# A state-space layer and a mish MLP on one core: sine tables moved behind the second mish group, two mish products moved later, a ScalarE table loaded early, identity matmuls in the head's gaps, the last output in two parts

## Chip, cores, metric

One core of one Trainium2 chip. The metric is device time of one execution in microseconds (us), the median of several executions. The span of a profile is about 2 us shorter than the time of the same execution (before: 633.1 and 635.1 us), so spans are compared with spans and times with times.

## The reference

The input x has 2048 rows of 1024. It is normalised, and the result feeds two branches: a diagonal complex state-space recurrence, and an MLP with mish.

```python
def _A_ref(x, Lambda_re, Lambda_im, B_re, B_im, C_re, C_im, log_dt, Dskip):
    Lam = Lambda_re + 1j * Lambda_im
    Bmat = B_re + 1j * B_im
    Cmat = C_re + 1j * C_im
    Lam_bar = jnp.exp(jnp.exp(log_dt) * Lam)
    B_bar = ((Lam_bar - 1.0) / Lam)[:, None] * Bmat
    Bu = jnp.einsum("bld,pd->blp", x + 0j, B_bar)
    h = jnp.zeros_like(Bu[:, 0, :]); hs = []
    for t in range(L):
        h = Lam_bar[None, :] * h + Bu[:, t, :]
        hs.append(h)
    hseq = jnp.stack(hs, 1)
    return 2.0 * jnp.einsum("blp,dp->bld", hseq, Cmat).real + x * Dskip[None, None, :]

def _B_ref(x, w1, b1, w2):            # w1: 1024 x 3584
    h = jnp.einsum("bsd,df->bsf", x, w1) + b1
    sp = jnp.log1p(jnp.exp(-jnp.abs(h))) + jnp.where(h > 0, h, jnp.zeros_like(h))
    return jnp.einsum("bsf,fd->bsd", h * jnp.tanh(sp), w2)

xn = _layernorm(x, axis=-1)
out = x + _A_ref(xn, ...) + _B_ref(xn, ...)
```

## The kernel before

The kernel goes through four blocks of 512 rows. In each block TensorE does four stages:

1. w1: 28 tiles of 8 matmuls. VectorE evicts each tile to `hb` and adds the bias.
2. Projection with B: 8 tiles of 16 matmuls. VectorE evicts each by multiplying it with sine and cosine tables (`tab`), which turns the complex recurrence into a real one.
3. w2: 224 matmuls that accumulate in all eight PSUM banks.
4. Projection with C: 128 matmuls into the same banks. It needs the recurrences, which VectorE does meanwhile.

ScalarE computes mish in four groups of seven tiles: exp, ln, tanh over 3584 columns each. VectorE multiplies the result with `hb` (`mish_mul`), which also frees `hb` for later tiles. In the first block there is extra work: layernorm without a predecessor to hide behind (the head), the sine tables, and the coefficients.

In the traces here each of these engines starts its operations in the order in which the program lists them: in the kernel before, the first mish exp (39.09 us) starts only behind the third sine table (35.65 us) that the code lists before it. So the place of a call in the code is read below as its place in its engine's queue.

```python
NWARM = 34
for i in range(NWARM):            # identity matmuls, result not used
    PE.mm(lambda e: e.matmul(ps[:, 4, 0:P], lhsT=ident[:], rhs=ident[:], start=True, stop=True), ...)
PE.op(lambda e: e.transpose(ps16(5)[:, 0:NST], st[:, :], ident[0:NST, 0:NST]), ...)   # parameters
for h in range(2):
    first_sums_v(0, h)            # VectorE: statistics of rows 0 to 127 (quarter 0)
first_var_v(0)
vop(lambda e: e.tensor_copy(par[:, :], ps16(5)[:, 0:NST]), ...)
first_mean_a(1)                   # ScalarE: mean of quarter 1
first_rsqrt(0)                    # ScalarE
first_var_a(1)
first_rsqrt(1)
first_sums_v(2, 0)
first_apply(0)                    # VectorE: Newton step, then xn
first_transpose(0)                # TensorE
first_apply(1)
first_transpose(1)
first_copy(0, VE)                 # PSUM to xnT
first_mean_a(3)
first_var_a(3)
first_rsqrt(3)
first_copy(1, AC)                 # on ScalarE
# ... quarters 2 and 3
for f in range(NSPLIT):           # first halves (256 columns) of w1 tiles 0 to 5
    first_half(f, 0)
    if f in (1, 3):
        q = 2 + f // 2
        first_transpose(q)
        first_copy(q, AC if q == 2 else VE)
# ... POOL: phases(j), the arguments of the sines, one j after the other

def table(j):                     # ScalarE
    src, b_src = ph_slot(j)       # written by POOL
    aop(lambda e: e.activation(tab[:, 1, j, :], src[:], AF.Sin, ...), ...)
    aop(lambda e: e.activation(src[:], src[:], AF.Abs), ...)
    aop(lambda e: e.activation(tab[:, 0, j, :], src[:], AF.Sin, ...), ...)

def first_tile(blk, f):           # ... matmuls of w1 tile f
    if f % GF == 0 and f >= 2 * GF:
        mish_mul(f // GF - 2)     # VectorE
    vop(lambda e: e.tensor_scalar(hb[:, hs, :], ps[:, bank, :], b1(f), None, op0=ALU.add), ...)
    if f % GF == GF - 1:
        mish(f // GF)             # ScalarE

def project_in(blk):
    for j in range(NJ):           # banks 4-5, 6-7, 0-1, 2-3, and again
        # ... 16 matmuls, two multiplications with tab, a sum and a difference on VectorE
        if j == 4:
            mish_mul(2)
        if j == 7:
            mish_mul(3)

def tail(blk):
    # ... w2: six f for banks 4 to 7 first, then all; C; then for each quarter q:
    vop(lambda e, q=q, xr=xr: e.tensor_tensor(xr, ps[:, 2 * q:2 * q + 2, :]..., xr, op=ALU.add), ...)
    AC.dma(lambda e, xr=xr, r0=r0: e.dma_start(out[0, r0:r0 + P, :], xr), ...)

def side(f):                      # first block, behind w1 tile f
    if f == 5:
        for j in range(3):
            table(j)
    if f == 13:
        for j in range(3, NJ):
            table(j)
    # ... coefficients, next block's layernorm
    if f < 16 and f % 2 == 0:
        transpose_B(f // 2)       # transposed loads, SP's queue
    if f >= 16:
        transpose_C(f - 16)
```

Of the kernel before, what the change touches and what calls it, by code (L numbers as in the profile page):

```python
# [5 lines left out]
ALU = mybir.AluOpType  # L6
AF = mybir.ActivationFunctionType
DT = mybir.dt

P = 128  # L10
# [146 lines left out]
def build_kernel(nc, A_x, A_Lambda_re, A_Lambda_im, A_B_re, A_B_im, A_C_re, A_C_im,  # L157
# [24 lines left out]
        return nc.alloc_sbuf_tensor(name, shape, dtype)  # L182


    NWARM = 34
    NRING = 7
    ring = sb("ring", [P, NRING, 2048], bf16)
    b_ring = [Buf("ring%d" % i) for i in range(NRING)]
# [18 lines left out]
    tab = sb("tab", [P, 2, NJ, TB], bf16)  # L207
    b_tab = [Buf("tab%d" % j) for j in range(NJ)]
    xx = sb("xx", [P, 2, NQ, D], bf16)
    b_xx = [[Buf("xx%d_%d" % (i, q)) for q in range(NQ)] for i in range(2)]  # L210
    s_xx = [[DmaSem(nc, "d_xx%d_%d" % (i, q)) for q in range(NQ)] for i in range(2)]
    xn = sb("xn", [P, NQ, D], bf16)
    b_xn = [Buf("xn%d" % q) for q in range(NQ)]
# [37 lines left out]
    def ps16(i):  # L251
        return ps[:, i, :].bitcast(bf16)
# [86 lines left out]
    def first_sums_v(q, h):  # L339
        s = q // 2  # L340
        vop(lambda e: e.bn_stats(stats[:, s, h, :], xx[:, 0, q, h * 512:(h + 1) * 512]),
            reads=[b_xx[0][q]], writes=[b_stats[s]])
# [37 lines left out]
    def first_transpose(q):  # L380
        bank = 6 + q % 2
        for k in range(NK):
            PE.mm(lambda e, k=k: e.transpose(ps16(bank)[:, k * P:(k + 1) * P], xn[:, q, k * P:(k + 1) * P], ident[:]),
                  reads=[b_xn[q], b_ident], writes=[b_ps[bank]], first=k == 0, last=k == NK - 1)

    def first_copy(q, queue):
        dst = xnT[:, :, q * P:(q + 1) * P]
        srcp = ps16(6 + q % 2).rearrange("p (k t) -> p k t", k=NK)
        if queue is AC:
            aop(lambda e: e.copy(dst, srcp), reads=[b_ps[6 + q % 2]], writes=[b_xnT[q]])  # L390
        else:
            vop(lambda e: e.tensor_copy(dst, srcp), reads=[b_ps[6 + q % 2]], writes=[b_xnT[q]])
# [60 lines left out]
            reads=[b_cs[in0]], writes=[b_cs[out_]])  # L453


    for i in range(NWARM):
        PE.mm(lambda e: e.matmul(ps[:, 4, 0:P], lhsT=ident[:], rhs=ident[:], start=True, stop=True),
              reads=[b_ident], writes=[b_ps[4]], first=i == 0, last=i == NWARM - 1)
    PE.op(lambda e: e.transpose(ps16(5)[:, 0:NST], st[:, :], ident[0:NST, 0:NST]),
          reads=[b_st, b_ident], writes=[b_ps[5]])  # L460
    for h in range(2):
        first_sums_v(0, h)
    first_var_v(0)
    vop(lambda e: e.tensor_copy(par[:, :], ps16(5)[:, 0:NST]), reads=[b_ps[5]], writes=[b_par])
    first_mean_a(1)
    first_rsqrt(0)
    first_var_a(1)
    first_rsqrt(1)
    first_sums_v(2, 0)
    first_apply(0)  # L470
    first_transpose(0)
    first_apply(1)
    first_transpose(1)
    first_copy(0, VE)
    first_mean_a(3)
    first_var_a(3)
    first_rsqrt(3)
    first_copy(1, AC)
    first_sums_v(2, 1)
    first_var_v(2)  # L480
    first_rsqrt(2)
    first_apply(2)
    first_apply(3)
    NSPLIT = 6

    def first_half(f, half):
# [8 lines left out]

    for f in range(NSPLIT):
        first_half(f, 0)
        if f in (1, 3):
            q = 2 + f // 2
            first_transpose(q)  # L500
            first_copy(q, AC if q == 2 else VE)

# [145 lines left out]
    def project_in(blk):  # L648
        for j in range(NJ):
            bank = banks_of(j)  # L650
            for ci in range(2):
                for k in range(NK):
                    PE.mm(lambda e, j=j, ci=ci, k=k, bank=bank: e.matmul(  # L653
                        ps[:, bank + ci, :], lhsT=BT[:, ci, j, k, :], rhs=xnT[:, k, :], start=k == 0, stop=k == NK - 1),
                        reads=[b_BT[j]] + b_xnT, writes=[b_ps[bank + ci]], first=k == 0, last=k == NK - 1)
            u = ps[:, bank:bank + 2, :]
            for s in range(2):
                vop(lambda e, s=s, u=u, j=j: e.tensor_tensor(  # L658
                    mt[:, s, :, :], u, tab[:, s, j, :].unsqueeze(1).to_broadcast([P, 2, TB]), op=ALU.mult),
                    reads=[b_ps[bank], b_ps[bank + 1], b_tab[j]], writes=[b_m[s]])  # L660
            vop(lambda e, j=j: e.tensor_tensor(hT[:, 0, j, :], mt[:, 0, 0, :], mt[:, 1, 1, :], op=ALU.add),
                reads=b_m, writes=[b_hT[0][j]])
            vop(lambda e, j=j: e.tensor_tensor(hT[:, 1, j, :], mt[:, 0, 1, :], mt[:, 1, 0, :], op=ALU.subtract),
                reads=b_m, writes=[b_hT[1][j]])
            if j == 4:
                mish_mul(2)
            if j == 7:
                mish_mul(3)

    def recur(blk, j):  # L670
# [30 lines left out]
    def tail(blk):  # L701
        first = [True] * 8

        def acc(u, lhsT, rhs, reads, last=False):
            st_ = first[u]
            first[u] = False
            PE.mm(lambda e: e.matmul(ps[:, u, :], lhsT=lhsT, rhs=rhs, start=st_, stop=last),  # L707
                  reads=reads, writes=[b_ps[u]], first=st_, last=last)

        def dense(f, s, units):  # L710
            wt = ring[:, s, :].rearrange("p (f d) -> p f d", f=2)
            for u in units:
                q, h = u // 2, u % 2
                acc(u, act[:, f, q * P:(q + 1) * P], wt[:, f % 2, h * TB:(h + 1) * TB], [b_actf[f], b_ring[s]])

        def proj(j, ci, u, last):
            q, h = u // 2, u % 2
            acc(u, hT[:, ci, j, q * P:(q + 1) * P], CT[:, ci, j, h * TB:(h + 1) * TB], [b_hT[ci][j], b_CT[j]], last)

        njt = 1 if blk == 0 else 3  # L720
        base = n_item[0]
        for f in range(6):
            dense(f, (base + f // 2) % NRING, (4, 5, 6, 7))
        for f in range(NF):
            dense(f, (base + f // 2) % NRING, (0, 1, 2, 3) if f < 6 else range(8))
            if f % 2 == 1:
                item_done()
            if blk + 1 < NB and f in (7, 9, 11, 13):
                transpose_dma((f - 7) // 2)
        for j in range(NJ - njt):  # L730
            for ci in range(2):
                for u in range(8):
                    proj(j, ci, u, False)
        i = blk % 2
        for q in range(NQ):
            for j in range(NJ - njt, NJ):
                for ci in range(2):
                    for u in (2 * q, 2 * q + 1):
                        proj(j, ci, u, j == NJ - 1 and ci == 1)
            xr = xx[:, i, q, :]  # L740
            vop(lambda e, q=q, xr=xr: e.tensor_tensor(  # L741
                xr, ps[:, 2 * q:2 * q + 2, :].rearrange("p a t -> p (a t)"), xr, op=ALU.add),
                reads=[b_ps[2 * q], b_ps[2 * q + 1], b_xx[i][q]], writes=[b_xx[i][q]])
            r0 = blk * TB + q * P
            out_events[i, q] = AC.dma(lambda e, xr=xr, r0=r0: e.dma_start(out[0, r0:r0 + P, :], xr), s_out[i][q],
                                      reads=[b_xx[i][q]])
        if blk + 2 < NB:
            for q in range(NQ):
                load_x(PO, blk + 2, q)


    for blk in range(NB):
        def side(f):
            if blk:
                if f in (8, 10, 12, 15):
                    ln_skip(blk, (8, 10, 12, 15).index(f))
                return
            if f == 5:
                for j in range(3):
                    table(j)  # L760
            if f == 13:
                for j in range(3, NJ):
                    table(j)
            if f in (7, 8, 9, 10):
                coefficients(f - 7)
            if f in (9, 11, 12, 13):
                ln_skip(0, (9, 11, 12, 13).index(f))
            if f in (14, 16, 18, 20):
                ln_stats_only(1, (f - 14) // 2)
            if f == 22:  # L770
                ln_rsqrt()
            if f in (23, 24, 25, 26):
                ln_scale(1, f - 23)
            if f < 16 and f % 2 == 0:
                transpose_B(f // 2)
            if f >= 16:
                transpose_C(f - 16)

        for f in range(NF):
            first_tile(blk, f)  # L780
            side(f)
        if blk == 0:
            for i in range(12, 2 * NK):
                transpose_C(i)
        project_in(blk)
        if 0 < blk < NB - 1:
            for q in range(NQ):
                ln_stats_only(blk + 1, q)
            ln_rsqrt()
            for q in range(NQ):  # L790
                ln_scale(blk + 1, q)
        for j in range(NJ):
            recur(blk, j)
            if blk == 0:
                scale_C(j)
        if blk + 1 < NB:
            carry()
        tail(blk)
# [51 lines left out]
```

## Time and profile before

634.95 us (634.46 to 635.81, 3 runs). TensorE is busy nearly throughout; these are the first two lines of section 1 of the page (span; busy us, share of the span, instructions):

```profile
span 633.1 us, 7295 instructions
PE 614.8 (97%) x2875; PEld 286.8 (45%) x2931; DVE 463.6 (73%) x693; ACT 249.6 (39%) x163; POOL 48.5 (8%) x47
```

The Trainium skill ("Trainium Kernel Development and Optimization", Performance Expectations) calls matmul busy time a bad metric, because matmuls are pipelined. Here one matmul's record is 0.379 us long, but they start 0.2158 us apart. This is the timeline of TensorE in the kernel before (start, length of a run of like instructions, source line, operands, count; in brackets the idle time before and what ended it):

```profile
8.70 1.03 PE L383 MATMUL ps<-ident,xn 128*128 128x128 bf16 x8 [2.67 <-DVE rs L369]
10.21 1.04 PE L383 MATMUL ps<-ident,xn 128*128 128x128 bf16 x8 [0.48 <-DVE xn L376]
12.81 3.57 PE L491 MATMUL ps<-xnT,ring 128*128 128x256 bf16 x16 [1.56 <-ACT xnT L390]
16.18 0.87 PE L383 MATMUL ps<-ident,xn 128*128 128x128 bf16 x8
...
19.08 7.15 PE L491 MATMUL ps<-xnT,ring 128*128 128x256 bf16 x64
26.28 27.57 PE L633 MATMUL ps<-xnT,ring 128*128 128x512 bf16 x125
54.40 1.89 PE L633 MATMUL ps<-xnT,ring 128*128 128x512 bf16 x8 [0.55 <-issue]
56.55 8.81 PE L633 MATMUL ps<-xnT,ring 128*128 128x512 bf16 x39 [0.26 <-DVE hb L640]
65.19 1.89 PE L653 MATMUL ps<-xnT,BT 128*128 128x512 bf16 x8
67.47 3.63 PE L653 MATMUL ps<-xnT,BT 128*128 128x512 bf16 x16 [0.39 <-DVE hb L640]
71.88 22.39 PE L653 MATMUL ps<-xnT,BT 128*128 128x512 bf16 x101 [0.79 <-DVE hb L640]
94.11 0.59 PE L707 MATMUL ps<-ring,act 128*128 128x512 bf16 x2
96.44 5.35 PE L707 MATMUL ps<-ring,act 128*128 128x512 bf16 x24 [1.73 <-DVE mt L658]
102.95 42.91 PE L707 MATMUL ps<-ring,act 128*128 128x512 bf16 x194 [1.15 <-DVE mt L658]
145.69 27.79 PE L707 MATMUL ps<-CT,hT 128*128 128x512 bf16 x125
```

Read it from above. Two of the four layernorm transposes (L383) come late and slowly, 1.03 us for eight. The first 16 half-width matmuls (L491) take 0.21 us each; later ones take 0.11. The slow ones run at half clock ("cold" below, against the full, "warm" clock): the packed trace's first record of the full clock is at 16.71 us, in the run of transposes that starts at 16.18. Some counts are a few short (125 of 128), because matmul records can be missing. All gaps of TensorE behind the head are in this list; they end at 102.95 us.

The cause of the gaps in the w1 stage stands on ScalarE and VectorE (timeline of the kernel before):

```profile
35.65 0.72 ACT L523 ACTIVATE tab<-ph_h,kon 128x512 bf16<-128x512 f32 x1 [2.94 <-POOL ph_h L517]
...
37.80 1.28 ACT L611 ACT_TABLE_LOAD   x1
39.09 3.19 ACT L611 ACTIVATE act<-hb 128x3584 bf16<-128x3584 bf16 x1
...
51.32 2.12 DVE L618 TENSOR_TENSOR act<-act,hb 128x3584 bf16<-128x3584 bf16 x1 [5.28 <-ACT act L613]
```

The third sine table waits for POOL's phases until 35.65. The first mish group's exp (L611) stands behind it in ScalarE's queue and starts at 39.09. So VectorE waits 5.28 us for the first mish product (L618), and every eviction behind that is late.

Two single lines complete the picture: the second ScalarE table load in the head, and the last add of the kernel, behind which the last output still has to land.

```profile
5.75 1.28 ACT L362 ACT_TABLE_LOAD   x1
...
629.36 1.23 DVE L741 TENSOR_TENSOR xx<-ps,xx 128x1024 bf16<-128x1024 f32 x1 [1.37 <-PE ps L707]
```

### The profile page before, as it was taken

How to read it: one execution, taken by the hardware profiler on the slowest of the kernel's cores; microseconds unless marked ns; L12 is line 12 of the kernel's file. 1: busy time of each engine (PE TensorE's matmuls, PEld its weight loads, DVE VectorE, ACT ScalarE, POOL GpSimd, SP SyncE). 2: the span in 40 equal slices, each digit the busy share in tenths (PEclk: the TensorE clock that was granted, in tenths of full speed). 3: DMA queues.
4: the chain of work that ended last, by engine and by line, in shares of the span. 5: the costliest groups of instructions: out<-in, count | busy, mean ns of one | idle time of the engine just before them, and what ended most of it. 6: DMA issues, size and time to landing. Idle time of an engine off the chain costs nothing.

```text
span 633.1 us, 7295 instructions
## 1 busy us (share of the span) xinstructions
PE 614.8 (97%) x2875; PEld 286.8 (45%) x2931; DVE 463.6 (73%) x693; ACT 249.6 (39%) x163; POOL 48.5 (8%) x47
## 2 busy tenths in 40 slices
PE   5999998999999999999999999999999999999997
PEld 4744443444444444444444444444444444444443
DVE  5587999999558579999145759999714756999603
ACT  6489996442029980000006994000000999000000
POOL 1699000000010000000010000000000000000000
PEclk9999999999999999999999999999999999999999
DMA  9999992852074500575045540186304442032001
GB/s 256 214 221 232 267 191 87 215 164 67 17 237 147 165 35 0 161 206 161 6 154 155 155 134 1 38 217 179 99 30 133 139 164 67 1 132 101 0 1 66
DMA packets 124043, 79.39 MB, mean 125 GB/s; under 512 B 48874, under 2 KB 106218, under 8 KB 124010
## 3 DMA queue, kind: packets, MB, share of 16 engines
q1 hardware_dynamic: 120656, 71.58, 42.6%
q10 hardware_dynamic: 2394, 4.21, 1.8%
q0 software_dynamic: 960, 3.15, 1.8%
q8 instruction: 23, 0.38, 0.2%
q14 instruction: 10, 0.08, 0.1%
HBM read 63.19 MB, written 4.19 MB: 106 GB/s over the span
## 4 chain that ended last, share of the span: by engine, by line
PE 84%; DVE 6%; ACT 5%; POOL 2%; issue 1%; DMA 0%; SPq 0%; DVEq 0%; POOLq 0%
PE ps L707 48%; PE ps L633 21%; PE ps L653 14%; DVE mt L658 2%; ACT act L613 1%; ACT act L611 1%; ACT act L612 1%; DVE hb L640 1%; POOL py L515 1%; PE ps L491 1%; POOL px L513 1%; DVE act L618 1%; POOL ph_h L517 1%; DMA xx<-in_A_x_dram 0%; ACT L612 0%
## 5 line engine op out<-in xcount | busy, mean ns | idle before, releaser
L707 PE MATMUL ps<-ring,act 128*128 128x512 bf16 x880 | 193.5, 379 | 3.7 <-DVE mt L658 2.9
L633 PE MATMUL ps<-xnT,ring 128*128 128x512 bf16 x832 | 183.0, 379 | 1.6 <-issue 0.5
L611 ACT ACTIVATE act<-hb 128x3584 bf16<-128x3584 bf16 x16 | 50.9, 3182 | 238.3 <-DVE hb L640 238.0
L707 PEld LDWEIGHTS ps<-ring,act 128*128 128x128 bf16 x896 | 87.5, 98 | 109.1 <-DVE mt L658 3.9
L633 PEld LDWEIGHTS ps<-xnT,ring 128*128 128x128 bf16 x848 | 82.8, 98 | 101.1 <-issue 1.0
L640 DVE TENSOR_SCALAR hb<-ps,par 128x512 bf16<-128x512 f32 x112 | 82.8, 747 | 56.3 <-PE ps L633 54.3
L653 PE MATMUL ps<-xnT,BT 128*128 128x512 bf16 x500 | 110.7, 379 | 1.8 <-DVE hb L640 1.2
L707 PE MATMUL ps<-CT,hT 128*128 128x512 bf16 x500 | 110.5, 379 | 0.6
L658 DVE TENSOR_TENSOR mt<-ps,tab 128x1024 bf16<-128x1024 f32 x64 | 75.3, 1218 | 13.1 <-PE ps L653 11.6
L653 PEld LDWEIGHTS ps<-xnT,BT 128*128 128x128 bf16 x512 | 49.9, 98 | 61.9 <-DVE hb L640 1.9
L707 PEld LDWEIGHTS ps<-CT,hT 128*128 128x128 bf16 x512 | 50.1, 98 | 60.4
L741 DVE TENSOR_TENSOR xx<-ps,xx 128x1024 bf16<-128x1024 f32 x16 | 19.3, 1223 | 72.8 <-PE ps L707 72.8
L673 DVE TENSOR_TENSOR_SCAN hT<-cs,qi,hT 128x512 bf16<-128x512 f32 x48 | 58.9, 1267 | 0.0
L612 ACT ACTIVATE act<-act 128x3584 bf16<-128x3584 bf16 x16 | 51.0, 3190 | 0.2
L613 ACT ACTIVATE act<-act 128x3584 bf16<-128x3584 bf16 x16 | 51.0, 3190 | 0.2
L678 DVE TENSOR_TENSOR mt<-hT,tab 128x1024 bf16<-128x1024 bf16 x64 | 41.4, 688 | 1.1
L618 DVE TENSOR_TENSOR act<-act,hb 128x3584 bf16<-128x3584 bf16 x16 | 32.6, 2040 | 6.6 <-ACT act L613 6.6
L287 POOL DMA_DIRECT2D xx<-in_A_x_dram x12 | 6.7, 560 | 260.9 <-DVE xx L741 255.6
L587 ACT ACTIVATE ct<-CT,cs 128x512 f32<-128x512 bf16 x16 | 11.5, 720 | 31.6 <-DVE CT L589 28.4
L612 ACT ACT_TABLE_LOAD x16 | 20.5, 1283 | 0.3
L613 ACT ACT_TABLE_LOAD x16 | 20.5, 1283 | 0.3
L673 DVE TENSOR_TENSOR_SCAN hT<-cs,hT 128x512 bf16<-128x512 f32 x16 | 18.7, 1208 | 0.0
(82 smaller groups left out, 277.1 us busy)
## 6 DMA issues: line engine op xcount, KB each, us to landing
ring<-in_B_w_dram SPq DMA_DIRECT2D x112, 512.0 KB, 3.8
out_dram<-xx ACTq DMA_DIRECT2D x16, 256.0 KB, 2.0
xx<-in_A_x_dram POOLq DMA_DIRECT2D x12, 256.0 KB, 5.2
xx<-in_A_x_dram SPq DMA_DIRECT2D x4, 256.0 KB, 3.7
dsk<-in_A_Dskip_dram SPq DMA_DIRECT2D x1, 256.0 KB, 6.4
xnT<-xn SPq DMA_TRANSPOSE x12, 4.5
BT<-in_A_B_re_dram SPq DMA_TRANSPOSE x8, 6.1
BT<-in_A_B_im_dram SPq DMA_TRANSPOSE x8, 4.1
```

Source lines behind the costliest of these rows:

```text
L611: aop(lambda e: e.activation(a, hs, AF.Exp), reads=[b_hb[g % 2]], writes=[b_act[g]])
L612: aop(lambda e: e.activation(a, a, AF.Ln, bias=1.0), reads=[b_act[g]], writes=[b_act[g]])
L613: aop(lambda e: e.activation(a, a, AF.Tanh), reads=[b_act[g]], writes=[b_act[g]])
L618: vop(lambda e: e.tensor_tensor(a, a, hs, op=ALU.mult), reads=[b_act[g], b_hb[g % 2]], writes=[b_act[g]])
L633: PE.mm(lambda e, k=k: e.matmul(ps[:, bank, :], lhsT=wt[:, k, fi * P:(fi + 1) * P], rhs=xnT[:, k, :], start=k == 0, stop=k == NK - 1), rea ...
L640: vop(lambda e: e.tensor_scalar(hb[:, hs, :], ps[:, bank, :], b1(f), None, op0=ALU.add), reads=[b_ps[bank], b_par], writes=[b_hbf[hs]])
L653: PE.mm(lambda e, j=j, ci=ci, k=k, bank=bank: e.matmul(ps[:, bank + ci, :], lhsT=BT[:, ci, j, k, :], rhs=xnT[:, k, :], start=k == 0, stop= ...
L658: vop(lambda e, s=s, u=u, j=j: e.tensor_tensor(mt[:, s, :, :], u, tab[:, s, j, :].unsqueeze(1).to_broadcast([P, 2, TB]), op=ALU.mult), rea ...
L673: vop(lambda e, ci=ci, init=init: e.tensor_tensor_scan(out=hT[:, ci, j, :], data0=cj("r", j).to_broadcast([P, TB]), data1=hT[:, ci, j, :], ...
L678: vop(lambda e, s=s: e.tensor_tensor(mt[:, s, :, :], hT[:, :, j, :], tab[:, s, j, :].unsqueeze(1).to_broadcast([P, 2, TB]), op=ALU.mult), ...
L707: PE.mm(lambda e: e.matmul(ps[:, u, :], lhsT=lhsT, rhs=rhs, start=st_, stop=last), reads=reads, writes=[b_ps[u]], first=st_, last=last)
L741: vop(lambda e, q=q, xr=xr: e.tensor_tensor(xr, ps[:, 2 * q:2 * q + 2, :].rearrange("p a t -> p (a t)"), xr, op=ALU.add), reads=[b_ps[2 * ...
```

## The change

Its parts, each with its intent:

- an operation on constants at the start loads the ScalarE table that rsqrt needs while x is still coming (the other layernorm functions are in it too);
- 16, 6 and 8 identity matmuls fill gaps between the transposes, to keep TensorE's clock up;
- the parameter copy leaves the front of VectorE's queue; the second transpose's copy goes to VectorE; the transposes of quarters 2 and 3 move by one or no tile;
- all eight sine tables go behind the second mish group, so that the first group need not wait for POOL;
- in the first block the third mish product moves from behind projection tile 4 to behind tile 6, and the fourth from behind tile 7 to behind the first recurrence;
- the last output unit is finished in two halves.

```diff
-    for i in range(NWARM):
-        PE.mm(...identity...)
+    def keep_busy(n):
+        for i in range(n):
+            PE.mm(...identity...)
+
+    keep_busy(34)
     PE.op(lambda e: e.transpose(ps16(5)[:, 0:NST], st[:, :], ident[0:NST, 0:NST]), ...)
+    keep_busy(16)
+    aop(lambda e: e.activation(rs[:, :, 3], kon[:, 2:3].to_broadcast([P, NQ]), AF.Abs_reciprocal_sqrt, bias=kon[:, 2:3]),
+        reads=[b_kon], writes=b_rs)
     for h in range(2):
         first_sums_v(0, h)
     first_var_v(0)
-    vop(lambda e: e.tensor_copy(par[:, :], ps16(5)[:, 0:NST]), reads=[b_ps[5]], writes=[b_par])
+    first_sums_v(2, 0)
     first_mean_a(1)
     first_rsqrt(0)
     first_var_a(1)
     first_rsqrt(1)
-    first_sums_v(2, 0)
     first_apply(0)
     first_transpose(0)
+    keep_busy(6)
     first_apply(1)
     first_transpose(1)
+    keep_busy(8)
     first_copy(0, VE)
+    first_copy(1, VE)
     first_mean_a(3)
     first_var_a(3)
     first_rsqrt(3)
-    first_copy(1, AC)
     ...
     first_apply(3)
+    vop(lambda e: e.tensor_copy(par[:, :], ps16(5)[:, 0:NST]), reads=[b_ps[5]], writes=[b_par])
     ...
-        if f in (1, 3):
-            q = 2 + f // 2
+        if f in (2, 3):
+            q = f
     ...
-            if j == 4:
+            if j == (6 if blk == 0 else 4):
                 mish_mul(2)
-            if j == 7:
+            if j == 7 and blk:
                 mish_mul(3)
     ...
         for q in range(NQ):
-            (all matmuls of both banks, one add of 1024 columns, one output DMA)
+            units = [(2 * q, 2 * q + 1)]
+            if blk == NB - 1 and q == NQ - 1:
+                units = [(2 * q,), (2 * q + 1,)]
+            (per unit: its matmuls, its add, its output DMA)
     ...
-            if f == 5:
-                for j in range(3):
-                    table(j)
             if f == 13:
-                for j in range(3, NJ):
+                for j in range(NJ):
                     table(j)
     ...
             recur(blk, j)
+            if blk == 0 and j == 0:
+                mish_mul(3)
```

More of the change, by code (lines that the diff above doesn't have):

```diff
@@ L182, in sb @@
         return nc.alloc_sbuf_tensor(name, shape, dtype)
-    NWARM = 34
     NRING = 7
@@ L209, in build_kernel @@
     xx = sb("xx", [P, 2, NQ, D], bf16)
-    b_xx = [[Buf("xx%d_%d" % (i, q)) for q in range(NQ)] for i in range(2)]
+    b_xx = [[Buf("xx%d_%d" % (i, q), parts=[Buf("xx%d_%d_%d" % (i, q, h)) for h in range(2)])
+             for q in range(NQ)] for i in range(2)]
     s_xx = [[DmaSem(nc, "d_xx%d_%d" % (i, q)) for q in range(NQ)] for i in range(2)]
@@ L453, in smalls @@
             reads=[b_cs[in0]], writes=[b_cs[out_]])
-    for i in range(NWARM):
-        PE.mm(lambda e: e.matmul(ps[:, 4, 0:P], lhsT=ident[:], rhs=ident[:], start=True, stop=True),
-              reads=[b_ident], writes=[b_ps[4]], first=i == 0, last=i == NWARM - 1)
+    def keep_busy(n):
+        for i in range(n):
+            PE.mm(lambda e: e.matmul(ps[:, 4, 0:P], lhsT=ident[:], rhs=ident[:], start=True, stop=True),
+                  reads=[b_ident], writes=[b_ps[4]], first=i == 0, last=i == n - 1)
+    keep_busy(34)
     PE.op(lambda e: e.transpose(ps16(5)[:, 0:NST], st[:, :], ident[0:NST, 0:NST]),
           reads=[b_st, b_ident], writes=[b_ps[5]])
+    keep_busy(16)
+    aop(lambda e: e.activation(rs[:, :, 3], kon[:, 2:3].to_broadcast([P, NQ]), AF.Abs_reciprocal_sqrt, bias=kon[:, 2:3]),
+        reads=[b_kon], writes=b_rs)
     for h in range(2):
@@ L734, in tail, with finish @@
         i = blk % 2
-        for q in range(NQ):
-            for j in range(NJ - njt, NJ):
-                for ci in range(2):
-                    for u in (2 * q, 2 * q + 1):
-                        proj(j, ci, u, j == NJ - 1 and ci == 1)
-            xr = xx[:, i, q, :]
-            vop(lambda e, q=q, xr=xr: e.tensor_tensor(
-                xr, ps[:, 2 * q:2 * q + 2, :].rearrange("p a t -> p (a t)"), xr, op=ALU.add),
-                reads=[b_ps[2 * q], b_ps[2 * q + 1], b_xx[i][q]], writes=[b_xx[i][q]])
-            r0 = blk * TB + q * P
-            out_events[i, q] = AC.dma(lambda e, xr=xr, r0=r0: e.dma_start(out[0, r0:r0 + P, :], xr), s_out[i][q],
-                                      reads=[b_xx[i][q]])
+        def finish(q, lo, hi):
+            xr = xx[:, i, q, lo:hi]
+            bank, r0 = 2 * q + lo // TB, blk * TB + q * P
+            b_x = b_xx[i][q].parts[lo // TB] if hi - lo <= TB else b_xx[i][q]
+            if hi - lo > TB:
+                src, b_src = ps[:, bank:bank + 2, :].rearrange("p a t -> p (a t)"), b_ps[bank:bank + 2]
+            else:
+                src, b_src = ps[:, bank, lo % TB:lo % TB + hi - lo], b_ps[bank:bank + 1]
+            vop(lambda e: e.tensor_tensor(xr, src, xr, op=ALU.add), reads=b_src + [b_x], writes=[b_x])
+            sem = s_out[i][q] if hi - lo > TB else DmaSem(nc, "d_end%d" % lo)
+            out_events[i, q, lo] = AC.dma(lambda e: e.dma_start(out[0, r0:r0 + P, lo:hi], xr), sem, reads=[b_x])
+        for q in range(NQ):
+            units = [(2 * q, 2 * q + 1)]
+            if blk == NB - 1 and q == NQ - 1:
+                units = [(2 * q,), (2 * q + 1,)]
+            for us in units:
+                for j in range(NJ - njt, NJ):
+                    for ci in range(2):
+                        for u in us:
+                            proj(j, ci, u, j == NJ - 1 and ci == 1)
+                if len(us) == 1:
+                    finish(q, (us[0] % 2) * TB, (us[0] % 2 + 1) * TB)
+            if len(units) == 1:
+                finish(q, 0, D)
         if blk + 2 < NB:
```

## The prediction

> **What bounds the kernel now.** TensorE. The page gives PE 97% of a 633.1 us span, clock 9 tenths or more throughout; the chain of waits is 84% PE. A block has 704 matmuls of 512 columns; in the chain's steady stretches 50 take 10.79 us (49 are recorded), 215.8 ns each, so the 2816 need 607.7 us. The other 25.4 us are all there is to win (estimate from the PE timeline):
> - head: first real matmul at 12.81 us;
> - cold clock: the first 16 half-width matmuls take 3.57 us, later ones 0.112 each: 1.7 lost; identity transposes 1.3;
> - PE gaps in the first block: 0.55 and 0.26 (54 to 57 us), 0.39 and 0.79 (67 to 72), 1.73 and 1.15 (94 to 103); 4.9 us, about 5.9 with a pipeline drain each;
> - end: 3.7 from the last matmul (629.36).
> Blocks 1 to 3 have no gaps.
>
> **The change, costed.**
> 1. Head. ScalarE's chain decides it (mean, variance, rsqrt up to 11.77 in the chain of waits). Its second table load (5.75, 1.28 us) stands before rsqrt; the change loads once, at 2.49, while x is coming. The Trainium skill, "ScalarE: Activation LUTs", What ACT_TABLE_LOAD costs, gives 1283 ns; the trace agrees. VectorE no longer waits 0.62 us for the parameter copy, and the second transpose's copy moves from ScalarE (queued to 11.68, 0.99 us) to VectorE (0.68). First matmul at 10.9: -1.9.
> 2. Identity matmuls. The Trainium skill, "TensorE: Matmul & The Clock Gate", Part 1, says the full clock comes after about 3.4 us of sustained activity; here it comes at about 16.4, 3.6 us after 12.81. If the fillers hold PE busy from 5.8 to 10.9, the first halves run warm: -1.7. First halves end near 17.3 instead of 20.85: -3.5 together.
> 3. Sine tables. Three tables wait for POOL's phases (25.5, 30.5, 35.6), so the first mish group starts at 37.8 though its input is ready at 28.7. VectorE then idles 5.28 us at the first mish product (51.3), later evictions are late, and the gaps at 54 to 57 and 67 to 72 follow. After: mish 0 at 25 to 37, mish 1 to 53, eight tables (2.03 each) to 71, mish 2 and 3 to 96 (before 100.6). These four gaps should vanish: -2.6.
> 4. The third product (2.02 us at 92.1) stands between two projection evictions and causes the gaps at 94 to 103. Moved later: -2.2, about 0.9 left, since VectorE (3.26 us per tile against 3.45 on PE) starts late.
> 5. End: the last add is 1.23 us on 1024 columns; half of it hides: -0.6.
>
> Against it: w1 loads in the first block are near the DMA's limit (DMA share about 1 from 24 to 66 us). The last is issued at 54.98 and needed at 61.7; PE will want it near 57. The DMA stream starts up to 2.9 us earlier (SP waited that long at 22.8), so 0 to 1.5 us may come back as a wait for DMA. The block-1 x loads may hold VectorE a little. I take off 0.8.
>
> Sum: -3.5 -2.6 -2.2 -0.6 +0.8 = -8.1.
>
> **Predicted: 627.0 us (range 624.8 to 630.2).** Faster by over 2%: 0.02; within 2%: 0.97; slower: 0.01.
>
> **What would show it.** First w1 matmul near 10.9; its 16 halves in about 1.9 us; one table load before the exp; first mish exp near 25; no VectorE idle over 3 us at the first product; w1 stage ending near 60.5 instead of 65.2; PE gaps in the first block under 1.5 us; a last add near 0.65.
>
> **What would make it wrong.** The fillers do not reach the warm clock (+1.7) or delay the transposes; PE waits for w1 loads or for VectorE's backlog (up to +3); the third product now delays the last projection evictions. All gaps gone would give 625.

## The result, and the profile after

626.04 us (625.92 to 626.63, 4 runs), against 634.98 us before (634.46 to 635.81, 4 runs). The ratio is 0.986, 95% interval 0.9843 to 0.9877. The profiled span is 623.9 us, 9.2 us shorter.

Section 1 of the page, and the timeline of TensorE after:

```profile
span 623.9 us, 7415 instructions
PE 616.7 (99%) x2961; PEld 287.4 (46%) x2961; DVE 466.0 (75%) x695; ACT 247.1 (40%) x162; POOL 50.0 (8%) x47
```

```profile
7.41 0.62 PE L383 MATMUL ps<-ident,xn 128*128 128x128 bf16 x8 [0.50 <-DVE rs L369]
7.87 0.50 PE L458 MATMUL ps<-ident 128*128 128x128 bf16 x6
8.77 0.62 PE L383 MATMUL ps<-ident,xn 128*128 128x128 bf16 x8 [0.40 <-DVE xn L376]
9.23 0.61 PE L458 MATMUL ps<-ident 128*128 128x128 bf16 x8
10.27 2.78 PE L499 MATMUL ps<-xnT,ring 128*128 128x256 bf16 x24 [0.43 <-DVE xnT L392]
...
21.64 38.15 PE L641 MATMUL ps<-xnT,ring 128*128 128x512 bf16 x176
59.62 27.79 PE L661 MATMUL ps<-xnT,BT 128*128 128x512 bf16 x128
87.25 5.78 PE L715 MATMUL ps<-ring,act 128*128 128x512 bf16 x26
94.55 42.91 PE L715 MATMUL ps<-ring,act 128*128 128x512 bf16 x198 [1.52 <-DVE mt L666]
137.29 27.79 PE L715 MATMUL ps<-CT,hT 128*128 128x512 bf16 x128
```

The transposes take 0.62 us instead of 1.03 (the clock is up), and the first weight matmul starts at 10.27. The w1 stage and the B projection run without a gap. One gap is left behind the head, 1.52 us in front of 94.55.

The other engines' lines that answer to those shown of before:

```profile
2.43 1.28 ACT L465 ACT_TABLE_LOAD   x1 [2.43 <-issue]
...
24.35 3.19 ACT L619 ACTIVATE act<-hb 128x3584 bf16<-128x3584 bf16 x1 [4.74 <-DVE hb L648]
...
41.33 2.01 DVE L626 TENSOR_TENSOR act<-act,hb 128x3584 bf16<-128x3584 bf16 x1
...
90.21 2.02 DVE L626 TENSOR_TENSOR act<-act,hb 128x3584 bf16<-128x3584 bf16 x1
92.14 2.35 DVE L666 TENSOR_TENSOR mt<-ps,tab 128x1024 bf16<-128x1024 f32 x2
...
620.96 0.69 DVE L752 TENSOR_TENSOR xx<-ps,xx 128x512 bf16<-128x512 f32 x1 [0.60 <-PE ps L715]
```

The first mish exp starts at 24.35 instead of 39.09. VectorE reaches the first product at 41.33 and finds it ready. The third product runs at 90.21, and behind it the eviction of the last projection tile ends at 94.49 (92.14 plus 2.35); TensorE goes on at 94.55. The last add is 0.69 us.

The difference splits at the starts of the stages, all read from the two timelines:

| stretch | before, us | after, us | difference | predicted |
|---|---|---|---|---|
| start to the first weight matmul | 12.81 | 10.27 | -2.54 | -1.9 |
| from there to the first full-width w1 matmul | 13.47 | 11.37 | -2.10 | -1.7 |
| w1 | 38.91 | 37.98 | -0.93 | -2.6 with the next |
| projection with B | 28.92 | 27.63 | -1.29 | |
| w2 of the first block | 51.58 | 50.04 | -1.54 | -2.2 |
| C of the first block to the last add | 483.67 | 483.67 | 0.00 | 0 |
| last add to the end | 3.74 | 2.94 | -0.80 | -0.6 |
| PE waiting for w1 loads, given back | | | 0 | +0.8 |
| sum | | | -9.20 | -8.1 (rounded) |

The time was inside the range. What the terms don't show is why the middle three moved, and whether the head's parts add up. The experiments are about that.

### The profile page after: what moved, and what is told of

Same layout as the page of the kernel before. It is cut to its first block, busy times and chain, and to the rows that moved or that the text cites. A ratio compares the mean times of both kernels' runs of the same rounds, so it can differ in the third digit from the quotient of the medians.

```text
span 623.9 us, 7415 instructions
## 1 busy us (share of the span) xinstructions
PE 616.7 (99%) x2961; PEld 287.4 (46%) x2961; DVE 466.0 (75%) x695; ACT 247.1 (40%) x162; POOL 50.0 (8%) x47
## 4 chain that ended last, share of the span: by engine, by line
PE 95%; DVE 3%; DMA 1%; issue 0%; SPq 0%; DVEq 0%
PE ps L715 48%; PE ps L641 29%; PE ps L661 16%; DVE mt L666 2%; PE ps L499 2%; DMA xx<-in_A_x_dram 1%; DVE hT L669 0%; PE ps L383 0%; DVE hT L671 0%; DVE xn L376 0%; SPq L287 0%; DVE xnT L392 0%; DVE xx L752 0%; DVE rs L371 0%; DVE stats L341 0%
## 5 line engine op out<-in xcount | busy, mean ns | idle before, releaser
L752 DVE TENSOR_TENSOR xx<-ps,xx 128x1024 bf16<-128x1024 f32 (+1 forms) x17 | 19.5, 1161 | 72.0 <-PE ps L715 72.0
L620 ACT ACT_TABLE_LOAD x16 | 20.5, 1283 | 0.3
L621 ACT ACT_TABLE_LOAD x16 | 20.5, 1283 | 0.3
```

Source lines behind the costliest of these rows:

```text
L620: aop(lambda e: e.activation(a, a, AF.Ln, bias=1.0), reads=[b_act[g]], writes=[b_act[g]])
L621: aop(lambda e: e.activation(a, a, AF.Tanh), reads=[b_act[g]], writes=[b_act[g]])
L752: vop(lambda e: e.tensor_tensor(xr, src, xr, op=ALU.add), reads=b_src + [b_x], writes=[b_x])
```

## The experiments

Two theories of the middle, from the first w1 matmul at full width to the first C matmul (119.41 us before, 115.65 after: -3.76):

- **P**, as predicted: the sine tables account for the w1 and B stretches; the moved products account for the w2 stretch.
- **R**, formed from the trace after: TensorE waits last for the eviction of the last projection tile (banks 2 and 3). That eviction is at the end of a queue in which VectorE never idles (the trace of after has no wait of VectorE from 62 to 96 us), so only the amount of work ahead of it and the moment at which VectorE gets to it count. The third product is ahead of the last tile at its old place and at its new one. Then the tables account for everything.

Each run was timed beside the kernel before (medians of the same rounds 635.1 to 635.6 us). All were correct. Differences "in the trace" compare profiled spans or stretches of them.

| run | edit to | median, us (range) | ratio to before (95%) | profiled span |
|---|---|---|---|---|
| tables_back | after | 631.00 (630.84 to 633.26) | 0.9943 (0.992 to 0.9965) | 629.1 |
| tables_only | before | 631.41 (631.26 to 632.16) | 0.9941 (0.9927 to 0.9956) | 630.2 |
| products_back | after | 626.59 (626.02 to 626.92) | 0.9862 (0.9847 to 0.9877) | 623.9 |
| no_fill | after | 628.72 (627.90 to 629.63) | 0.9897 (0.9882 to 0.9912) | 625.9 |
| no_load | after | 628.27 (627.68 to 628.78) | 0.9889 (0.9874 to 0.9904) | 626.4 |
| fill_only | before | 634.05 (633.18 to 634.99) | 0.9981 (0.9965 to 0.9997) | 633.0 |
| load_only | before | 633.48 (633.03 to 634.08) | 0.9973 (0.9959 to 0.9988) | 632.1 |
| copy_back | after | 627.09 (627.00 to 632.09) | 0.9897 (0.9854 to 0.9939) | 625.0 |
| no_split | after | 627.60 (627.10 to 628.17) | 0.9879 (0.9865 to 0.9894) | 626.0 |
| after_again | none | 626.01 (625.95 to 626.29) | 0.9857 (0.984 to 0.9873) | 624.0 |
| product_late | after | 625.03 (624.19 to 626.45) | 0.9842 (0.9824 to 0.986) | 622.6 |
| late_and_loads | after | 624.51 (624.17 to 624.78) | 0.983 (0.9816 to 0.9843) | 622.2 |

### tables_back: the tables at their old places in the kernel after

```diff
+            if f == 5:
+                for j in range(3):
+                    table(j)
             if f == 13:
-                for j in range(NJ):
+                for j in range(3, NJ):
                     table(j)
```

> The kernel after, with three sine tables again before the first mish group and five after the second. Two theories of the gain between the first full-width w1 matmul and the first projection of C (3.8 us in the traces). Theory R, formed from the trace of after: all of it comes from the tables, since what PE waits for last is the last projection tile's eviction, and that is late only because VectorE's w1 evictions were; then +3.8 us, span about 627.7, and a PE gap of 3 us or more in all before the last projection banks. Theory P, as predicted: the tables give only the gaps at 54 to 57 and 67 to 72 us, so +2.2 us, span about 626.1, and the rest stays with the moved products.

The middle took 120.22 us instead of 115.65 (22.33 to 142.55 in its timeline): +4.57. The gaps of the w1 and B stages are back (1.31, 0.26, 0.39 and 0.78 us), and the gap in front of the last banks is 2.92 us. That is more than even R said, and far from P's 2.2. The surplus has a likely source, which these two numbers suggest and no run tests. The shorter head does not shorten POOL's chain as much: ScalarE gets the third table's phases 10.22 us behind the first full-width matmul here and 9.37 us in the kernel before (32.55 less 22.33; 35.65 less 26.28). So in the shortened head the old order would have cost more than it did. The rest of the 5.2 us of span is a first full-width matmul that came 0.69 us later in this execution. The slowest of the four runs (633.26 us) was not traced.

### tables_only: the tables alone moved in the kernel before

> The kernel before, with all eight sine tables behind the second mish group and nothing else changed (the products stay at their old places). Theory R (the tables carry the whole gain of the middle): PE gaps between 54 and 72 us gone, and those before the last projection banks down to about 1.5 us in sum: -3.8 us, span about 629.3. Theory P, as predicted (tables -2.6, the moved products the rest): -2.6 us or less, span 630.5 or more.

The edit is the reverse of the one above. The middle took 115.86 us (26.88 to 142.74) instead of 119.41: -3.55 of the -3.76, with the products at their old places. The gaps of the w1 and B stages are gone, and those before the last banks are 0.62 and 1.15 us. The time fell by 3.9 us. R holds; P is outside.

### products_back: the products at their old places in the kernel after

```diff
-            if j == (6 if blk == 0 else 4):
+            if j == 4:
                 mish_mul(2)
-            if j == 7 and blk:
+            if j == 7:
                 mish_mul(3)
     ...
-            if blk == 0 and j == 0:
-                mish_mul(3)
```

> The kernel after, with the third and fourth mish products of the first block at their old places (after projection tiles 4 and 7). Theory P, as predicted: the third product again stands before the eviction of tile 5, and PE loses about 1.5 us more: span about 625.4. Theory R: the third product is before the last tile's eviction at either place, so the evictions end at the same time; the PE gap before the last banks is split in two (about 0.6 and 0.9 us) but its sum stays 1.5 us: span 623.9, within 0.2.

The profiled span is 623.9 us, as after, and the median is 0.5 us higher with overlapping ranges. TensorE goes on with banks 2 and 3 at the same moment as after (94.63 here, 94.55 after). These are the two lines of TensorE around it, and VectorE's third product and last tile's eviction, from the timelines:

```profile
87.40 6.07 PE L715 MATMUL ps<-ring,act 128*128 128x512 bf16 x26
94.63 42.91 PE L715 MATMUL ps<-ring,act 128*128 128x512 bf16 x194 [1.16 <-DVE mt L666]
...
83.78 2.02 DVE L626 TENSOR_TENSOR act<-act,hb 128x3584 bf16<-128x3584 bf16 x1
...
92.22 2.35 DVE L666 TENSOR_TENSOR mt<-ps,tab 128x1024 bf16<-128x1024 f32 x2
```

The product starts 6.43 us earlier than after (83.78 against 90.21), and the last eviction ends at 94.57 against 94.49. So in the traces moving the products, as the change does it, is worth nothing, and Theory P's term for it was wrong. Not traced are the other three executions, with spans of 624.6 to 624.8 us, where seven of the eight executions of after (its repeat included) have 623.9 to 624.2; whether their heads or the products made that is open. What R said in detail is half shown: the recorded gap is 1.16 us instead of 1.52, and the 26 matmuls ahead of it take 6.07 us instead of 5.78, which is where the first of R's two gaps would be.

### no_fill: without the added identity matmuls

```diff
-    keep_busy(16)
-    keep_busy(6)
-    keep_busy(8)
```

(each at its place; the 34 stay)

> The kernel after, without the 16, 6 and 8 added identity matmuls. My theory (the fillers bring the full clock before the first weight matmul): the first 16 half-width matmuls are cold again (about 3.5 us instead of 1.9) and the transposes take about 1.0 us instead of 0.62, so about +2.1 us against the kernel after (span about 626.0). Rival (the 34 old identity matmuls and the earlier start of work warm the clock anyway, the head's gain is ScalarE's alone): within 0.3 us of the kernel after.

The first 24 half-width matmuls took 4.43 us instead of 2.78, the first two groups of transposes 1.03 each instead of 0.62, and the first weight matmul came at 10.66. Span +2.0, median +2.7. In the packed traces the first record of the full clock is at 14.08 us here and at 6.48 after. The fillers do bring the clock. The rival is out.

### no_load: without the early table load

```diff
-    aop(lambda e: e.activation(rs[:, :, 3], ..., AF.Abs_reciprocal_sqrt, bias=kon[:, 2:3]), ...)
```

> The kernel after, without the early ScalarE operation that loads layernorm's table. My theory: a second table load of 1.28 us returns in front of the first rsqrt, and everything behind it in the head moves: first weight matmul at about 11.5 instead of 10.27, +1.3 us (span about 625.2), more only if the longer hole between fillers and transposes costs the clock. Rival (the fillers and VectorE's order made the head's gain; the load hides behind the wait for x): within 0.3 us of the kernel after.

The first rsqrt started at 6.98 instead of 5.62 us, so the load costs 1.36 us. But the first weight matmul moved by 1.73 us and the span by 2.5, and the clock was lost on the way (timeline of TensorE; its idle times are called holes below):

```profile
8.63 0.62 PE L383 MATMUL ps<-ident,xn 128*128 128x128 bf16 x8 [1.35 <-DVE rs L369]
9.09 0.50 PE L458 MATMUL ps<-ident 128*128 128x128 bf16 x6
10.15 0.98 PE L383 MATMUL ps<-ident,xn 128*128 128x128 bf16 x8 [0.56 <-DVE xn L376]
10.92 1.06 PE L458 MATMUL ps<-ident 128*128 128x128 bf16 x8
12.00 3.58 PE L497 MATMUL ps<-xnT,ring 128*128 128x256 bf16 x24
```

The first transposes are still fast. Behind holes of 1.35 and 0.56 us the second ones are slow, the fillers take 1.06 us for 8, and the 24 halves begin slowly. The record of the granted clock agrees: it is 0.50 from 10.25 to 13.66 us and full before and after. In these traces, then, the table load and the fillers work together: the load shortens the hole in front of the first transposes from 1.35 to 0.50 us. That the holes cause the fall is an inference; copy_back below kept the clock over a hole of 1.53 us.

### fill_only and load_only: each alone in the kernel before

> The kernel before, with the 16, 6 and 8 identity matmuls and nothing else changed. Theory of the window (the clock falls back when the holes between them are too long, as the run without the early table load showed with a hole of 1.35 us): the holes stay long here, so only part of the cold time is saved: -0.3 to -1.2 us, and the second transposes take about 1.0 us again. Rival (the fillers' worth does not depend on the rest): -2.0 us, as much as taking them from the kernel after cost.

> The kernel before, with the early load of layernorm's ScalarE table and nothing else changed. If the load's 1.28 us stand on the head's chain by themselves: first weight matmul at about 11.5 instead of 12.81, -1.3 us, the first 16 half-width matmuls still cold at 3.57. Rival (VectorE's wait for the parameter copy, 0.62 us, or ScalarE's queue takes it back): -0.7 us or less.

Fillers alone: in the profiled run the hole in front of the first transposes is 1.72 us, the second transposes take 1.04 us and the first 16 halves 3.57, exactly as before, so nothing was saved in it (span 633.0). The clock had come at 6.54 us, fell to 0.50 at 9.95 and returned at 16.78. The four spans fall in two pairs, 631.2 and 631.3, 632.8 and 633.0. The better pair was not traced; that the clock held longer in it is an inference, and the mean clocks don't separate the pairs (0.996 twice; 0.995 and 0.997). The median is 1.3 us lower: short of the rival's -2.0, and also just outside the theory's -1.2. Two of the four runs (633.18 and 633.36 us) did save the rival's 2 us. So the interaction is shown in the traced execution only; the fillers alone help in some executions and not in others.

The load alone: first weight matmul at 11.38 (-1.43), the halves cold at 3.57. The median fell by 1.6 us and the profiled span by 1.0. That the span fell by less than the head fits the clock, which came 5.04 us behind the first weight matmul in that run (16.42) and 3.90 behind it in before; the second 16 halves took 2.31 us instead of 1.91. As expected; the rival is out.

### copy_back: the second copy on ScalarE again

```diff
     first_copy(0, VE)
-    first_copy(1, VE)
     ...
     first_rsqrt(3)
+    first_copy(1, AC)
```

> The kernel after, with the second transpose's copy on ScalarE behind the fourth quarter's rsqrt again. As predicted (the copy's own 0.31 us and its place in ScalarE's queue): first weight matmul at about 11.4 instead of 10.27, +1.1 us; if the hole that this leaves behind the fillers (about 1.5 us) loses the clock, up to +2. Rival (the copy is not what the first matmul waits for): 0.

First weight matmul at 11.42 (+1.15), span 625.0 (+1.1), median +1.05. The hole of 1.53 us behind the fillers did not lose the clock this time: the 24 halves took 2.78 us. One of the four runs took 632.09 us; it has no trace here, so its cause is open.

The head's parts don't add up to its gain. Taken out of after, one at a time, the fillers, the load and the copy cost 2.7, 2.2 and 1.05 us in medians, 6.0 together, and the whole head gained 4.64 us in the traces: the same clock is counted in more than one of them. The new places of the parameter copy and of the transposes were not tested alone.

### no_split: the last output in one piece

```diff
-            if blk == NB - 1 and q == NQ - 1:
+            if False:
```

> The kernel after, with the last output unit in one piece again. As predicted: the last add is 1.23 us instead of 0.69 behind the last matmul, +0.6; with the larger last transfer (2.0 us to landing instead of 1.7) +0.8, as the traces of before and after differ at the end; span about 624.7. Rival (the end is bound by the transfers in the queue before it): 0.

From the last add's start to the end it took 3.80 us (622.20 to 626.0) instead of 2.94, so the split is worth 0.86 us. The whole span is 2.1 us longer, not 0.8. The rest is another head: in this execution the third quarter of x came late (VectorE waited 0.82 us for it), the clock came late (first record of the full clock at 10.84 us, 6.48 after), and the first weight matmul was at 11.50. Such differences of the head between executions are a reason to read a part's worth from its own stretch.

### after_again, product_late, late_and_loads: the last gap

R says that the remaining gap of 1.52 us goes if the third product stands behind the last tile.

```diff
-            if j == (6 if blk == 0 else 4):
+            if j == (7 if blk == 0 else 4):
                 mish_mul(2)
```

> The kernel after, unchanged, as the measure for the next run on the same chip: 626.0 us, ratio about 0.986.

> The kernel after, with the third mish product of the first block behind the last projection tile instead of behind tile 6. Theory R (PE waits for the end of the last tile's eviction, and the product's 2.02 us stand in front of it): the eviction ends 2 us earlier, about when PE comes to its banks, and the PE gap of 1.5 us there goes: -1.5 us against the kernel after (span about 622.4). Theory P (the product has to be out of the way of tile 5 only, as in the change): no gain, within 0.2 us.

The gap went: the traced span is 622.6 us (-1.3), and TensorE has no wait behind the head. The middle is 1.73 us shorter than after (136.05 less 22.13, against 115.65). The last tile's eviction now stands ahead of the product (93.75) and ends at 93.05:

```profile
90.69 2.36 DVE L666 TENSOR_TENSOR mt<-ps,tab 128x1024 bf16<-128x1024 f32 x2
```

But the four spans run from 622.2 to 624.4, and the intervals of the two ratios overlap. The repeated run of the unchanged kernel after tells why that may be (its timeline of TensorE):

```profile
21.96 31.03 PE L641 MATMUL ps<-xnT,ring 128*128 128x512 bf16 x141
53.34 3.63 PE L641 MATMUL ps<-xnT,ring 128*128 128x512 bf16 x15 [0.35 <-DMA ring<-in_B_w_dram]
57.89 3.63 PE L641 MATMUL ps<-xnT,ring 128*128 128x512 bf16 x16 [0.92 <-DMA ring<-in_B_w_dram]
88.98 48.57 PE L715 MATMUL ps<-ring,act 128*128 128x512 bf16 x220
```

This is the wait for w1 loads that the prediction took 0.8 us off for: 1.27 us in two waits. Yet the span is 624.0, as without it, for the gap in front of banks 2 and 3 is gone instead. TensorE came to those banks later, when VectorE was done. In the kernel after, VectorE's last projection tile decides, and a wait ahead of it of this size costs nothing. In product_late that cover is gone. The last run tests this: the third product late, and the transposed loads of B's last four tiles moved from in front of the last w1 loads to behind them (the loads of C that followed move back with them).

```diff
-            if f < 16 and f % 2 == 0:
+            if f < 8 and f % 2 == 0:
                 transpose_B(f // 2)
-            if f >= 16:
-                transpose_C(f - 16)
+            if 16 <= f < 20:
+                transpose_B(f - 12)
+            if f >= 20:
+                transpose_C(f - 20)
     ...
-            for i in range(12, 2 * NK):
+            for i in range(8, 2 * NK):
                 transpose_C(i)
```

> The kernel after with the third product behind the last projection tile, and with the transposed loads of B's last four tiles (issued behind w1 tiles 8, 10, 12, 14 before) moved behind w1 tiles 16 to 19, so that they no longer stand in the queue before the last w1 loads. The run with the late product alone spread from 624.2 to 626.5 us. If that spread is PE's wait for w1 loads in the first block, which the repeated run of after showed in its trace (1.3 us in two waits) and which is hidden there behind VectorE's last projection tile: no PE wait for w1 loads in the trace, span about 622.4, all runs within 0.6 us of 624.4. If the spread comes from elsewhere (the head's clock): the same spread as without it.

624.51 us, all five runs from 624.17 to 624.78. There is no wait for w1 loads in the trace, the span is 622.2, and the stages follow each other without a gap (w1 21.62 to 59.61, B to 87.24, w2 to 135.58). This version is ahead of both kernels: its range lies below that of after (625.92 to 626.63) and of after_again (625.95 to 626.29, on another chip). The ratio to before is 0.983. That its spread is narrow where product_late's was wide fits the w1 loads as the cause; product_late's slow executions themselves were not traced.

## Why the prediction was right, and where its steps were not

The time (626.04 for 627.0 predicted) and the frame held: TensorE bounds the kernel, everything to be won lies in the head, the first block and the end, and the other three blocks did not move (483.67 us both times).

1. **Head, first weight matmul, predicted -1.9, measured -2.54.** Mechanism right. The mis-sized term is the second copy. Beside the load's 1.28 us the sum had about 0.6 us for it and the parameter copy together; copy_back measured 1.15 for the second copy alone.
2. **Clock, predicted -1.7, measured -2.10** for the stretch to the first full-width matmul. The fillers bring and hold the clock (no_fill). What I did not see is that they can fail without the early load (no_load and the traced execution of fill_only). The Trainium skill ("TensorE: Matmul & The Clock Gate", Part 1) puts the warm-up at about 3.4 us of sustained activity and calls it run-variable; the runs agree: the 16 fillers took from 1.07 to 1.89 us in different executions of the same head. (In the kernel before, the clock's record puts the change at 16.71 us, 3.9 us after 12.81, not at 16.4.) Where the clock fell again it stayed at half for 3.41, 6.83 and 10.24 us (no_load, fill_only, tables_only), one, two and three times the same length.
3. **Sine tables, predicted -2.6, measured -2.22** on the w1 and B stretches, and the four gaps are gone as said. But the step "These four gaps should vanish" ended the account too early. The same late evictions also delayed VectorE's start on the projection tiles, so the tables were worth 3.55 us alone and 4.57 us when taken back.
4. **Products, predicted -2.2, measured -1.54 on that stretch, and not from them.** The step "The third product stands between two projection evictions and causes the gaps ... Moved later" is wrong as a cause. With the products at their old places the profiled span did not change (products_back). I took the operation that stood in front of the gap for its cause. What counts is when the last tile's eviction ends, and the product's 2.02 us were ahead of it in either place. Behind the last tile the third product costs TensorE no wait (product_late). That the sum of steps 3 and 4 came out near (4.8 predicted, 3.76 measured) is partly luck: what the products did not give, the tables gave in the w2 stretch.
5. **End, predicted -0.6, measured -0.80** (0.86 in no_split). The add gives 0.54 (1.23 less 0.69). The rest is behind the add: the halves land in 1.7 us, the full units in 2.0 (medians).
6. **Waits for w1 loads, predicted +0.8, measured 0 in time.** They do occur (1.27 us in after_again, none in the first profile) but were hidden by the wait named in 4.

## What to carry to other kernels

When an in-order engine is the last to be waited for, moving one of its operations earlier or later ahead of the awaited one changes nothing as long as the engine has no idle time there (here TensorE goes on at 94.55 and 94.63 us); moving it behind does. Start a queue's work on what is ready (here mish before tables that wait for a slow engine), and look for the gain not only in the gaps beside it but in the next stage that the same engine reaches late. Fillers that keep TensorE's clock up can fail when the holes between them are long, and not in every execution, so shorten the chain first and look at several executions. Read the worth of a part from its own stretch when heads differ from one execution to the next.

## What the Trainium skill lacked or had wrong

- "ScalarE: Activation LUTs", What ACT_TABLE_LOAD costs: it gives 1283 ns for the load and about 1380 ns more for a drain, 2.66 us for every switch. The load is 1.28 us here, but taking one away moved the next operation by 1.36 us (6.98 to 5.62) in the kernel after. The drain was not there to be won.
- "TensorE: Matmul & The Clock Gate", Back-to-back issue gap: it gives 131 ns as the sustained spacing of pairs of weight load and matmul with 512 columns, and 81 ns with 128. Here 128 such pairs took 27.63 us, 215.9 ns each, and 8 transposes with 128 columns 0.46 us from start to start (7.41 to 7.87), 57 ns each. The figures that Part 1 of the same page gives for back-to-back matmuls on the full clock (215.7 and 55.6) fit.
- The same page, HAM oscillation: its rule is to have no idle gap of over about 3.4 us. In no_load two holes of 1.35 and 0.56 us, with 14 transposes and fillers at full rate between them, were enough for the slow clock (0.50 from 10.25 us); in copy_back two of 0.57 and 1.53 us were not. So a sum of short holes can be too much, and whether it is varies; the rule for one gap does not tell it. The page's section on a second failure mode does say that frequent short idle times can make the clock swing, but gives no lengths.
- The clock page warns that throttle events in traces can be unreliable (Seeing it yourself, HAM trace caveats). Here they agree with the matmuls: in no_load the granted clock is 0.50 from 10.25 to 13.66 us, where the second transposes and the first halves are slow. What misleads is that the views print 1.00 where the trace holds no record yet, as from 12.81 to 16.18 us in before, where 256 columns took 0.21 us: its first record is at 16.71. None of the pages tells of such a default. There the spacing of the matmuls tells the clock.
